# A Fourier filter and bilinear layer on one core: first batch in full rows of d, output stored in two halves of tokens

## The chip, the cores and the metric

The kernel runs on one core of one Trainium2 chip. The time is device microseconds of one execution of the whole program. All data is float32, and the matmuls of the main part are made exact enough by splitting operands into a high and a low part.

## The reference, cut to what matters

```python
# x [8, 3072, 256], filt_r / filt_i [1537, 256], w_a / w_b [256, 1536], w_out [1536, 256]
X = np.fft.rfft(x, axis=1)
y = np.fft.irfft(X * (filt_r + 1j * filt_i), n=3072, axis=1)
y = y.reshape(8 * 3072, 256)
out = ((y @ w_a) * (y @ w_b)) @ w_out
```

The weights arrive as float64 bit patterns and are converted on the chip.

## The kernel before, in words

**Filter.** The transform of the 3072 tokens is done in two stages of matmuls (3072 = 128 x 24). Stage one of the first batch is `first_s1` (12 items), whose result goes to HBM in `z0`; it comes back in another layout (`first_z`), goes through stage two, the product with the filter and the first inverse stage (`first_s2` and `first_is1`, 16 turns), and is put into HBM in `td`. The last inverse stage (`is2`) reads it from there (tile `tt`) with a table `gt` and leaves the operand pair `ah`, `al` for 512 tokens, one chunk. The first batch has its own functions (`first_*`, L437 to L509), which work on halves of d: 12 items are 2 halves of 128 columns by 6 groups of four n, and 16 turns are 2 halves by 8 groups. Rows of 128 float32 (512 bytes) are what its transfers carry.

**Weights.** Eighteen pieces of the weights are loaded and split by a pipeline, `more_weights` (L653): one call, here named a tick, loads piece t and does the five later stages of the pieces before it. In the before kernel six ticks are called ahead of and inside the loop of `first_s1`, six in the loop over the turns, and eleven in the first slots of the main part.

**Main part.** Eight batches of six chunks c, each with twelve slots f (L764 to L788). A slot is numbered 12 * c + f in its batch. In each slot `hidden` makes two products of 512 tokens with 128 hidden columns, `product` multiplies them on DVE into `g`, and `project` multiplies by `w_out` with a seven-product scheme into PSUM tiles `po`. The work for the next batch and the next chunk (loads, transform stages) is put into slots by hand with `at(slot, fn, ...)`, L715 to L763. Two entries matter here: `load_t` for the first chunk of the next batch stands in slot 68, which is c = 5, f = 8, and the two `is2` that need it in slots 69 and 70 (L761 to L763); and in batch 0 `load_s` of item i + 2 stands in slot 14 + i, and `s1` of the same item two slots later (L738, L743). The order of instructions on an engine is the order in which this program calls them, and SP's queue, which issues nearly all loads, has one such order as well.

**Output.** When a chunk's products are complete, `combine_first` (f = 2) and `combine` (f = 3 of the next chunk) add them up into `ct`, and `store` (f = 5) transposes `ct` in 32 x 32 blocks on DVE into `ot` and issues sixteen DMAs of 32 KB each from SP. After the last chunk the same is done with nothing beside it (L789 to L797).

Of the kernel before, what the change touches and what calls it, by code (L numbers as in the profile page):

```python
# [19 lines left out]
N1, N2 = 128, 24  # L20
# [175 lines left out]
def fft_filter_bilinear_kernel(ctx: ExitStack, tc, x, filt, fny, wa, wb, wo, s1c, gc, fc, fl, ic, sc, s1f, ff, fi, out):  # L196
# [240 lines left out]
    side = [slice(0, 128), slice(128, 256)]  # L437

# [5 lines left out]
    def first_x(h, i):  # L444
        xt = fr.tile([128, 4, 128], F32, name="x0", tag="in", bufs=9)
        nc.sync.dma_start(out=xt, in_=x[0].rearrange("(p n) d -> p n d", n=N2)[:, 4 * i:4 * i + 4, side[h]])
        held["x0", h, i] = xt

    def first_s1(h, i):
        xt, sf = held.pop(("x0", h, i)), held["sf", i // 2]  # L450
        bank, tag = ((ps_h, "pa"), (ps_h, "pb"), (ps_o, "po0"), (ps_o, "po1"))[i % 4]
        ps = bank.tile([128, 4, 128], F32, name="ps", tag=tag)
        for n in range(4):
            nc.tensor.matmul(ps[:, n], sf[:, 4 * (i % 2) + n], xt[:, n], start=True, stop=True)
        z = fr.tile([128, 4, 128], F32, name="z0", tag="z0", bufs=3)
        nc.scalar.copy(out=z, in_=ps)
        nc.scalar.dma_start(out=z0[:, 4 * i:4 * i + 4, side[h]], in_=z)

    def first_f(h, i):
        ft = filts[(8 * h + i) % NFT].rearrange("p j (h d) -> p (j h) d", h=2)  # L460
        nc.sync.dma_start(out=ft, in_=filt[:, 4 * i:4 * i + 4, side[h]])
        held["f0", h, i] = ft

    def first_z(h, i):
        zt = fr.tile([128, 4, 128], F32, name="zf", tag="in", bufs=9)
        zv = z0.rearrange("(j q) n d -> j (q n) d", q=4)[4 * i:4 * i + 4, :, side[h]]
        nc.sync.dma_start(out=zt[0:96], in_=zv.rearrange("j p d -> p j d"))
        held["z0", h, i] = zt

    def first_turn(i, w, ins, ps):  # L470
        for j0, j1, kind in ((0, 1, 1), (1, 4, 0)) if i == 0 else ((0, 4, 0),):
# [3 lines left out]
    def first_s2(h, i):  # L475
        zt, ft = held.pop(("z0", h, i)), held.pop(("f0", h, i))
        bank, tag = ((ps_h, "pa"), (ps_h, "pb"), (ps_o, "po0"), (ps_o, "po1"))[i % 4]
        ps = bank.tile([128, 4, 128], F32, name="ps", tag=tag)
        first_turn(i, fcf, [zt[0:96]], ps)
        y = fr.tile([128, 4, 128], F32, name="y0", tag="y", bufs=3)  # L480
        v = fr.tile([128, 4, 128], F32, name="v0", tag="v", bufs=3)
        xi = fr.tile([128, 4, 128], F32, name="xi", tag="xi")
        nc.vector.tensor_tensor(out=y[0:64], in0=ps[0:64], in1=ft[0:64], op=ALU.mult)
        nc.vector.tensor_tensor(out=y[64:128], in0=ps[64:128], in1=ft[0:64], op=ALU.mult)
        nc.vector.tensor_tensor(out=v[64:128], in0=ps[0:64], in1=ft[64:128], op=ALU.mult)
        nc.scalar.mul(out=xi[64:128], in_=ps[64:128], mul=-1.0)
        nc.gpsimd.tensor_tensor(out=v[0:64], in0=xi[64:128], in1=ft[64:128], op=ALU.mult)
        if i == 0:
            nc.vector.tensor_tensor(out=y[64:65, 0], in0=ps[64:65, 0], in1=nyq[64:65, side[h]], op=ALU.mult)
        held["y0", h, i] = [y, v]  # L490

    def first_is1(h, i):
        ps = ps_f.tile([128, 4, 128], F32, name="ps", tag="ff")[0:96]
        first_turn(i, icf, held.pop(("y0", h, i)), ps)
        t = fr.tile([96, 4, 128], F32, name="t0", tag="t")
        nc.scalar.copy(out=t, in_=ps)
        tv = td[0].rearrange("(j q) n d -> j (q n) d", q=4)[4 * i:4 * i + 4, :, side[h]]
        nc.scalar.dma_start(out=tv.rearrange("j p d -> p j d"), in_=t)
# [9 lines left out]
    def first_tt(h):  # L508
        nc.sync.dma_start(out=held["t", 0, 0][0][:, :, side[h]], in_=td[0][:, 0:4, side[h]])  # L509
# [113 lines left out]
    def combine(b, c):  # L623
        (m5, m4), (m7, m6) = ((t[:, 0], t[:, 1]) for t in po.pop((b, c))[2:])
        ct, u1, u4, _ = sums.pop((b, c))
        u2 = moe[0].tile([128, 256], F32, name="u2", tag="u2")
        u3 = moe[0].tile([128, 256], F32, name="u3", tag="u3")
        for o, v, w, op in (
            (u2, m6, u1, ALU.add), (u3, m7, u2, ALU.add), (ct[:, 1, 0], u3, m4, ALU.subtract),
            (ct[:, 1, 1], m5, u3, ALU.add), (u2, m5, u2, ALU.add), (ct[:, 0, 1], u2, u4, ALU.add),  # L630
        ):
            nc.vector.tensor_tensor(out=o, in0=v, in1=w, op=op)
        sums[b, c] = ct

    def store(b, c):
        ct = sums.pop((b, c))

        ot = moe[0].tile([128, 16, 2, 32], F32, name="ot", tag="ot")
        for h in range(2):
            nc.vector.transpose(ot[:, :, h], ct[:, h].rearrange("p t (j c) -> p (t j) c", c=32))  # L640

        ov = out[S * b:S * b + S].rearrange("(j c n) d -> c n j d", j=4, c=32)[:, 4 * c:4 * c + 4]
        for i in range(4):
            for n in range(4):
                nc.sync.dma_start(  # L645
                    out=ov[:, n, :, 64 * i:64 * i + 64],
                    in_=ot[32 * i:32 * i + 32, 4 * n:4 * n + 4].rearrange("p j h r -> p j (h r)"),
                )


    with tc.manual_schedule():
# [9 lines left out]
        items = [(h, i) for h in range(2) for i in range(6)]  # L661
        turns = [(h, i) for h in range(2) for i in range(8)]
# [8 lines left out]
        for n in range(6, 8):  # L671
            first_x(*items[n])
        for n, item in enumerate(items):
            first_s1(*item)
            if n + 8 < len(items):
                first_x(*items[n + 8])
            if n == 4:
# [4 lines left out]
            if n in (1, 3):  # L682
                more_weights()
            if 5 <= n < 9:
                first_f(*turns[n - 5])
                first_z(*turns[n - 5])
            if n in (7, 10):
                more_weights()
        for n in range(NJ + 2):
            if n < NJ:  # L690
                first_s2(*turns[n])
            if n + 4 < NJ:
                first_z(*turns[n + 4])
            if NFT <= n + NFT - 1 < NJ:
                first_f(*turns[n + NFT - 1])
            if n >= 2:
                first_is1(*turns[n - 2])
            if n % 2 == 1 and tick[0] < 12:
                more_weights()
            if n == 13:  # L700
# [11 lines left out]
        for b in range(B):  # L712
# [6 lines left out]
            if b == 0:  # L719
# [4 lines left out]
                at(10, nc.sync.dma_start, s1d, s1c)  # L724
# [39 lines left out]
            for c in range(NC):  # L764
                for f in range(NF):
# [19 lines left out]
                    if f == 5 and last[0] >= 0:  # L785
                        store(*last)
# [9 lines left out]
        combine(*last)  # L796
        store(*last)  # L797
# [34 lines left out]
```

## Time and profile before

| | |
|---|---|
| median of 3 runs | 2778.95 us (2777.82 to 2781.3) |
| the profiled execution's own time | 2778.72 us |
| its span in the trace | 2776.9 us |
| mean granted TensorE clock | 0.984 |
| PE busy | 2686.4 us (97%) |
| DVE / ACT / POOL busy | 1653.3 (60%) / 1304.2 (47%) / 1645.5 us (59%) |
| PE in 40 slices | 6 7 7 8, then 9 in all but the last |

PE is TensorE; DVE, ACT and POOL are the vector, scalar and GpSimd engines, SP the engine whose queue issues the loads and stores. An entry "SPq" or "ACTq" is the issuing of a DMA. In a row of a timeline the number in square brackets is the idle time of the engine before the instruction, with what ended it. The PE clock has two levels, 1.2 and 2.4 GHz, shown as 0.50 and 1.00.

### The profile page before, as it was taken

The numbers are of one execution on the slowest core, as the hardware profiler recorded it, in microseconds if no ns is written. First come the engines' busy times: TensorE is split into PE (matmuls) and PEld (weight loads), VectorE is DVE, ScalarE is ACT, GpSimd is POOL, SyncE is SP. The second block draws the span as 40 slices with busy tenths as digits, with TensorE's granted clock in tenths as the row PEclk, the third lists the DMA queues.
The fourth block names the chain that finished last, engine by engine and source line by source line (L and its number), as shares of the span: only waits on it lengthen the run. The fifth ranks groups of instructions, "written<-read, shape, count | busy, mean of one in ns | idle before, by whom it ended". The sixth has DMA issues, their size and how long they took to land.

```text
span 2776.9 us, 43491 instructions
## 1 busy us (share of the span) xinstructions
PE 2686.4 (97%) x14926; PEld 2299.4 (83%) x14926; DVE 1653.3 (60%) x2673; ACT 1304.2 (47%) x2711; POOL 1645.5 (59%) x1419
## 2 busy tenths in 40 slices
PE   6778999999999999999999999999999999999997
PEld 3467888888888888888888888888888888888886
DVE  5765775457744577446764477545774457744443
ACT  3444444445445454454444444454454544444343
POOL 3576565666656566566666566565665656655554
PEclk8889999999999999999999999999999999999998
DMA  9526452445424443343433545144532444320110
GB/s 269 144 93 202 132 137 58 129 131 139 114 71 130 144 129 89 100 155 114 140 82 99 157 112 143 49 138 130 139 109 72 146 127 133 81 50 20 24 23 16
DMA packets 331233, 310.27 MB, mean 112 GB/s; under 512 B 130449, under 2 KB 258002, under 8 KB 330962
## 3 DMA queue, kind: packets, MB, share of 16 engines
q1 hardware_dynamic: 266354, 227.32, 30.1%
q10 hardware_dynamic: 64256, 79.71, 8.5%
q8 instruction: 118, 1.93, 0.3%
q14 instruction: 105, 0.86, 0.1%
q0 software_dynamic: 400, 0.44, 0.1%
HBM read 202.49 MB, written 108.00 MB: 112 GB/s over the span
## 4 chain that ended last, share of the span: by engine, by line
PE 85%; issue 3%; POOL 2%; DVE 1%; SPq 1%; DMA 1%; ACT 0%; POOLq 0%; DVEq 0%; ACTq 0%
PE pb L541 9%; PE pb L542 9%; PE pb L543 9%; PE pa L543 9%; PE pa L542 9%; PE pa L541 9%; PE po L600 8%; PE po L598 8%; PE po L599 8%; PE ps L524 3%; PE ps L364 2%; PE ps L399 2%; POOL gl L581 2%; PE ps L398 2%; SPq L645 1%
## 5 line engine op out<-in xcount | busy, mean ns | idle before, releaser
L581 POOL TENSOR_TENSOR gl<-g,gh 128x256 fp32r<-128x256 f32 x576 | 573.9, 1018 | 990.9 <-ACT gh L580 878.8
L551 DVE TENSOR_TENSOR g<-pb,a 128x512 f32<-128x512 f32 x576 | 398.2, 691 | 839.9 <-PE pb L543 436.0
L581 POOL TENSOR_TENSOR gl<-t,gh 128x512 fp32r<-128x512 f32 x576 | 754.0, 1331 | 32.2 <-ACT gh L580 32.2
L547 ACT COPY a<-pa 128x512 f32<-128x512 f32 x576 | 338.2, 587 | 495.3 <-PE pa L543 481.8
L600 PE MATMUL po<-gl,woh 128*128 128x256 f32 x2016 | 568.7, 282 | 1.2 <-POOL gl L581 1.2
L598 PE MATMUL po<-gh,woh 128*128 128x256 f32 x2016 | 568.5, 282 | 1.0 <-ACT gh L580 1.0
L599 PE MATMUL po<-gh,wol 128*128 128x256 f32 x2016 | 568.2, 282 | 0.0
L541 PE MATMUL pb<-ah,wbh 128*128 128x512 f32 x1152 | 462.0, 401 | 15.0 <-DVE g L551 13.3
L541 PE MATMUL pa<-ah,wah 128*128 128x512 f32 x1152 | 465.8, 404 | 6.4 <-ACT a L547 6.3
L542 PE MATMUL pb<-al,wbh 128*128 128x512 f32 x1152 | 457.9, 397 | 0.0
L543 PE MATMUL pa<-ah,wal 128*128 128x512 f32 x1152 | 457.6, 397 | 0.0
L542 PE MATMUL pa<-al,wah 128*128 128x512 f32 x1152 | 457.4, 397 | 0.0
L543 PE MATMUL pb<-ah,wbl 128*128 128x512 f32 x1152 | 457.4, 397 | 0.0
L580 ACT CAST gh<-t 128x512 fp32r<-128x512 f32 x576 | 328.6, 618 | 193.2 <-PE po L599 190.6
L598 PEld LDWEIGHTS po<-gh,woh 128*128 128x128 f32 x2016 | 380.0, 188 | 27.5 <-ACT gh L580 1.2
L599 PEld LDWEIGHTS po<-gh,wol 128*128 128x128 f32 x2016 | 380.5, 189 | 26.2
L600 PEld LDWEIGHTS po<-gl,woh 128*128 128x128 f32 x2016 | 381.3, 189 | 1.8 <-POOL gl L581 1.8
L541 PEld LDWEIGHTS pb<-ah,wbh 128*128 128x128 f32 x1152 | 218.1, 189 | 82.4 <-DVE g L551 28.9
L580 ACT CAST gh<-g 128x256 fp32r<-128x256 f32 x576 | 266.8, 513 | 0.0
L543 PEld LDWEIGHTS pb<-ah,wbl 128*128 128x128 f32 x1152 | 217.8, 189 | 53.6
L543 PEld LDWEIGHTS pa<-ah,wal 128*128 128x128 f32 x1152 | 217.8, 189 | 51.7
L542 PEld LDWEIGHTS pb<-al,wbh 128*128 128x128 f32 x1152 | 217.9, 189 | 50.4
(98 smaller groups left out, 3325.7 us busy)
## 6 DMA issues: line engine op xcount, KB each, us to landing
filt<-in_filt SPq DMA_DIRECT2D x336, 128.0 KB, 3.5
z<-zh ACTq DMA_DIRECT2D x112, 256.0 KB, 2.4
zt<-z SPq DMA_DIRECT2D x112, 256.0 KB, 3.0
td<-t ACTq DMA_DIRECT2D x128, 192.0 KB, 2.3
out<-ot SPq DMA_DIRECT2D x768, 32.0 KB, 1.6
tt<-td SPq DMA_DIRECT2D x47, 512.0 KB, 5.4
xt<-in_x SPq DMA_DIRECT2D x84, 256.0 KB, 3.2
st<-s1d SPq DMA_DIRECT2D x84, 256.0 KB, 4.3
```

The costliest lines, as they stand in the source:

```text
L364: nc.tensor.matmul(ps[:, n], st[:, n, w], m[:, n], start=q == 0, stop=q == 2)
L524: nc.tensor.matmul(ps[:, n], tt[:, n, 128 * k:128 * k + 128], gt[:, n], start=True, stop=True)
L541: nc.tensor.matmul(p, wh[:, k, fs], ah[:, k], start=k == 0, stop=False)
L542: nc.tensor.matmul(p, wh[:, k, fs], al[:, k], start=False, stop=False)
L543: nc.tensor.matmul(p, wl[:, k, fs], ah[:, k], start=False, stop=k == 1)
L547: nc.scalar.copy(out=a, in_=pa)
L551: nc.vector.tensor_tensor(out=raw[0][:, 2 * i:2 * i + 2].rearrange("p t n -> p (t n)"), in0=pb, in1=a, op=ALU.mult)
L580: nc.scalar.copy(out=gh[:, e], in_=g[:, e])
L581: nc.gpsimd.tensor_tensor(out=gl[:, e], in0=g[:, e], in1=f32(gh[:, e]), op=ALU.subtract)
L598: nc.tensor.matmul(o, woh[:, p, w], gh, start=first, stop=False, skip_group_check=True)
L599: nc.tensor.matmul(o, wol[:, p, w], gh, start=False, stop=False, skip_group_check=True)
L600: nc.tensor.matmul(o, woh[:, p, w], gl, start=False, stop=last, skip_group_check=True)
```

## The change

Three things change. First, the first batch works on full rows of d: an item is two n by 256 columns, a turn two j by 256, so that the same 12 items and 16 turns move rows of 1 or 2 KB, and the nyquist row is done once instead of twice. The loads of all items come ahead of the first weights; four ticks, not six, lie in the loop of the items, and eight in the loop of the turns. A turn now needs `z0` of all twelve items, where it needed that of six. `tt` of the first chunk is loaded by halves of its partitions, no longer by halves of d. Second, the two transposes and sixteen stores of a chunk are cut by halves of tokens t: two transposes of half the width and eight stores in slot f = 5, the same again in f = 7. Third, after the last chunk the first half is transposed and stored as soon as its sums are there, and the stores go alternately to SP's and ACT's queue.

```diff
-    def first_x(h, i):
-        xt = fr.tile([128, 4, 128], F32, name="x0", tag="in", bufs=9)
-        nc.sync.dma_start(out=xt, in_=x[0].rearrange("(p n) d -> p n d", n=N2)[:, 4 * i:4 * i + 4, side[h]])
...
+    def first_x(i):
+        xt = fr.tile([128, 2, D], F32, name="x0", tag="in", bufs=9)
+        nc.sync.dma_start(out=xt, in_=x[0].rearrange("(p n) d -> p n d", n=N2)[:, 2 * i:2 * i + 2])
...
+    def first_z(i):
+        zt = fr.tile([128, 2, D], F32, name="zf", tag="in", bufs=9)
+        zv = z0.rearrange("(j q) n d -> j (q n) d", q=4)[2 * i:2 * i + 2]
...
     def first_tt(h):
-        nc.sync.dma_start(out=held["t", 0, 0][0][:, :, side[h]], in_=td[0][:, 0:4, side[h]])
+
+        nc.sync.dma_start(out=held["t", 0, 0][0][half[h]], in_=td[0][half[h], 0:4])
...
-    def combine(b, c):
+    def combine(b, c, end=False):
...
             (u2, m6, u1, ALU.add), (u3, m7, u2, ALU.add), (ct[:, 1, 0], u3, m4, ALU.subtract),
+            (None, 0, 0, 0),
             (ct[:, 1, 1], m5, u3, ALU.add), (u2, m5, u2, ALU.add), (ct[:, 0, 1], u2, u4, ALU.add),
         ):
-            nc.vector.tensor_tensor(out=o, in0=v, in1=w, op=op)
-        sums[b, c] = ct
...
+            if o is not None:
+                nc.vector.tensor_tensor(out=o, in0=v, in1=w, op=op)
+            elif end:
+                store(b, c, ct, ot, 0, end)
+        sums[b, c] = ct, ot
+        if end:
+            store(b, c, ct, ot, 1, end)
+
+    def store(b, c, ct, ot, t, end=False):
+
         for h in range(2):
-            nc.vector.transpose(ot[:, :, h], ct[:, h].rearrange("p t (j c) -> p (t j) c", c=32))
+            nc.vector.transpose(ot[:, 8 * t:8 * t + 8, h], ct[:, h, t].rearrange("p (j c) -> p j c", c=32))
...
-        for i in range(4):
-            for n in range(4):
-                nc.sync.dma_start(
+        for n in (2 * t, 2 * t + 1):
+            for i in range(4):
+                (nc.scalar if end and i % 2 else nc.sync).dma_start(
...
-        for n in range(3):
+        for n in range(2):
             first_const(n)
-            first_x(*items[2 * n])
-            first_x(*items[2 * n + 1])
-        for n in range(2):
-            more_weights()
...
+            for i in range(4 * n, 4 * n + 4):
+                first_x(i)
+        first_const(2)
+        first_x(8)
...
-            if n in (1, 3):
+            if n in (2, 4, 6, 9):
                 more_weights()
...
+            if n in (7, 8):
+                first_f(n - 7)
+        for n in range(4):
+            first_z(n)
+            if n < 2:
+                first_f(n + 2)
...
-                at(10, nc.sync.dma_start, s1d, s1c)
+                at(7, nc.sync.dma_start, s1d, s1c)
...
-                    if f == 5 and last[0] >= 0:
-                        store(*last)
+                    if f in (5, 7) and last[0] >= 0:
+                        store(*last, *sums[last], f // 2 - 2)
...
-        combine(*last)
-        store(*last)
+        combine(*last, end=True)
```

At the passage from batch 0 to batch 1, DVE (`g` is the product of a slot, the three `t` are the differences of each odd slot, `ot` the transposes of the store, `al` the end of `is2`) has this order before, from f = 5 on:

```order
L640 STREAM_TRANSPOSE ot<-ct 128x16x32 x2
L551 TENSOR_TENSOR g<-pb,a 128x512 x2
L560 TENSOR_TENSOR t<-g 128x512
L561 TENSOR_TENSOR t<-g,t 128x256
L562 TENSOR_TENSOR t<-t,g 128x256
L551 TENSOR_TENSOR g<-pb,a 128x512 x2
L560 TENSOR_TENSOR t<-g 128x512
L561 TENSOR_TENSOR t<-g,t 128x256
L562 TENSOR_TENSOR t<-t,g 128x256
L527 TENSOR_TENSOR al<-ps,ah 128x512
```

and this one with the change:

```order
L646 STREAM_TRANSPOSE ot<-ct 128x8x32 x2
L552 TENSOR_TENSOR g<-pb,a 128x512 x2
L561 TENSOR_TENSOR t<-g 128x512
L562 TENSOR_TENSOR t<-g,t 128x256
L563 TENSOR_TENSOR t<-t,g 128x256
L646 STREAM_TRANSPOSE ot<-ct 128x8x32 x2
L552 TENSOR_TENSOR g<-pb,a 128x512 x2
L561 TENSOR_TENSOR t<-g 128x512
L562 TENSOR_TENSOR t<-g,t 128x256
L563 TENSOR_TENSOR t<-t,g 128x256
L528 TENSOR_TENSOR al<-ps,ah 128x512
```

Half of the transposes now stand behind the products and differences of f = 6 and 7. SP's queue at the same place, with the change:

```order
L651 DMA out<-ot 32x4x64 x16
L514 DMA tt<-td 128x1024
L516 DMA gt<-in_gc 128x512
L343 DMA xt<-in_x 128x2x256 x3
L348 DMA st<-s1d 128x512 x2
```

The row of sixteen stores reads as it did before, and `tt` and `gt` follow it as before; but its last eight now wait for the second pair of transposes.

In chunk 1 of batch 0, where the loads `xt` and `st` of the next batch are under way, SP's queue before is

```order
L348 DMA st<-s1d 128x512
L645 DMA out<-ot 32x4x64 x16
L343 DMA xt<-in_x 128x2x256
L348 DMA st<-s1d 128x512
L343 DMA xt<-in_x 128x2x256
L348 DMA st<-s1d 128x512
```

and with the change

```order
L348 DMA st<-s1d 128x512
L651 DMA out<-ot 32x4x64 x8
L343 DMA xt<-in_x 128x2x256
L348 DMA st<-s1d 128x512
L343 DMA xt<-in_x 128x2x256
L348 DMA st<-s1d 128x512
L651 DMA out<-ot 32x4x64 x8
```

Two pairs of loads now stand ahead of the second eight stores.

## Rows read from the trace of the kernel before

**Rows 1.** PE from 260 to 2750 us: busy time by stretch, then its waits there

```profile
260.00:2750.00 2490.00, 2481.13 (x14036) 2148.71 (x14035) 1485.45 (x2411) 1184.36 (x2483) 1492.88 (x1286) 1.00 0.37 106
...
PE pb L541 <- DVE g L551: 5.8, 15, 0.4
PE ps L524 <- DMA gt<-in_gc: 1.3, 3, 0.7
```

**Rows 2.** Timelines of SP, DVE and PE where batch 0 passes to batch 1

```profile
465.37 0.43 SPq L515 DMA_DIRECT2D gt<-in_gc  x1
...
462.18 0.43 DVE L562 TENSOR_TENSOR t<-t,g 128x256 f32<-128x256 f32 x1
...
469.98 1.13 PE L524 MATMUL ps<-gt,tt 128*128 128x128 f32 x8 [0.73 <-DMA gt<-in_gc]
```

**Rows 3.** The same timelines where batch 1 passes to batch 2

```profile
785.45 7.45 SPq L645 DMA_DIRECT2D out<-ot  x16
793.42 0.43 SPq L515 DMA_DIRECT2D gt<-in_gc  x1
...
791.57 0.42 DVE L562 TENSOR_TENSOR t<-t,g 128x256 f32<-128x256 f32 x1
...
798.48 1.05 PE L524 MATMUL ps<-gt,tt 128*128 128x128 f32 x8
```

**Rows 4.** Timeline of PE: first instructions after three of its idle times

```profile
127.59 0.80 PE L541 MATMUL pb<-ah,wbh 128*128 128x512 f32 x1 [3.56 <-DVE g L551]
...
155.19 0.50 PE L541 MATMUL pb<-ah,wbh 128*128 128x512 f32 x1 [1.40 <-DVE g L551]
...
190.22 0.50 PE L541 MATMUL pa<-ah,wah 128*128 128x512 f32 x1 [2.08 <-ACT a L547]
```

**Rows 5.** Stretches behind them: PE, PEld, DVE, ACT, POOL busy, PE clock, DMA share

```profile
132.00:133.00 1.00, 1.00 (x6) 0.86 (x5) 0.96 (x2) 0.00 (x0) 0.29 (x1) 0.58 0.89 172
155.00:156.00 1.00, 0.81 (x4) 0.69 (x5) 1.00 (x3) 0.97 (x3) 1.00 (x2) 1.00 0.00 0
191.00:192.00 1.00, 1.00 (x4) 0.71 (x4) 0.92 (x2) 0.00 (x0) 1.00 (x3) 0.50 0.00 0
194.00:195.00 1.00, 1.00 (x6) 0.82 (x6) 0.08 (x1) 0.15 (x1) 1.00 (x2) 0.86 1.17 360
```

**Rows 6.** Timelines of SP and PE in batch 0, chunk 1, around f = 5

```profile
223.77 8.02 SPq L645 DMA_DIRECT2D out<-ot  x16
232.38 0.41 SPq L348 DMA_DIRECT2D st<-s1d  x1
...
235.65 0.55 PE L364 MATMUL ps<-xh,st 128*128 128x256 f32 x1 [7.62 <-DMA st<-s1d]
```

**Rows 7.** The end: timeline of DVE and SP, then a stretch of the stores

```profile
2766.01 1.30 DVE L640 STREAM_TRANSPOSE ot<-ct 128x512 f32<-128x512 f32 x2
2767.35 7.43 SPq L645 DMA_DIRECT2D out<-ot  x16
...
2769.00:2771.00 2.00, 0.00 (x0) 0.00 (x0) 0.00 (x0) 0.00 (x0) 0.00 (x0) 0.50 0.41 66
```

**Rows 8.** Transfers of the first 40 us: GB/s by slice, and their packets

```profile
GB/s 0 45 152 383 323 252 241 347 345 359 350 306 365 416 404 367 343 332 307 271 294 324 280 344 395 372 358 354 205 116 310 225 229 251 240 261 319 374 390 349
DMA packets 16759, 11.90 MB, mean 297 GB/s; under 512 B 761, under 2 KB 15606, under 8 KB 16758
```

**Rows 9.** Timeline of DVE, then PE: turns 0, 3, 4 and 15 of the first batch, then `is2`

```profile
40.70 0.68 DVE L483 TENSOR_TENSOR y<-ps,filt 64x512 f32<-64x512 f32 x1
...
51.92 0.68 DVE L483 TENSOR_TENSOR y<-ps,filt 64x512 f32<-64x512 f32 x1
...
56.77 0.68 DVE L483 TENSOR_TENSOR y<-ps,filt 64x512 f32<-64x512 f32 x1
...
99.00 0.68 DVE L485 TENSOR_TENSOR v<-ps,filt 64x512 f32<-64x512 f32 x1
...
109.72 2.04 PE L524 MATMUL ps<-gt,tt 128*128 128x128 f32 x8 [5.83 <-DMA tt<-td]
```

More of the change, by code (lines that the diff above doesn't have):

```diff
@@ L434, in is1 @@
         nc.scalar.dma_start(out=tv.rearrange("j p d -> p j d"), in_=t)
-    side = [slice(0, 128), slice(128, 256)]
     def first_const(n):
@@ L459, in first_f @@
[L459 to L466, printed above, removed]
+    def first_x(i):
+        xt = fr.tile([128, 2, D], F32, name="x0", tag="in", bufs=9)
+        nc.sync.dma_start(out=xt, in_=x[0].rearrange("(p n) d -> p n d", n=N2)[:, 2 * i:2 * i + 2])
+        held["x0", i] = xt
@@ new lines, in fft_filter_bilinear_kernel, with first_s1 @@
+    BANKS = ((ps_h, "pa"), (ps_h, "pb"), (ps_o, "po0"), (ps_o, "po1"))
+    def first_s1(i):
+        xt, sf = held.pop(("x0", i)), held["sf", i // 4]
+        bank, tag = BANKS[i % 4]
+        ps = bank.tile([128, 2, D], F32, name="ps", tag=tag)
+        for n in range(2):
+            nc.tensor.matmul(ps[:, n], sf[:, 2 * (i % 4) + n], xt[:, n], start=True, stop=True)
+        z = fr.tile([128, 2, D], F32, name="z0", tag="z0", bufs=3)
+        nc.scalar.copy(out=z, in_=ps)
+        nc.scalar.dma_start(out=z0[:, 2 * i:2 * i + 2], in_=z)
@@ L467, in first_z, with first_f @@
+    def first_f(i):
+        ft = filts[i % NFT]
+        nc.sync.dma_start(out=ft, in_=filt[:, 2 * i:2 * i + 2])
+        held["f0", i] = ft
+    def first_z(i):
+        zt = fr.tile([128, 2, D], F32, name="zf", tag="in", bufs=9)
+        zv = z0.rearrange("(j q) n d -> j (q n) d", q=4)[2 * i:2 * i + 2]
         nc.sync.dma_start(out=zt[0:96], in_=zv.rearrange("j p d -> p j d"))
-        held["z0", h, i] = zt
+        held["z0", i] = zt
     def first_turn(i, w, ins, ps):
-        for j0, j1, kind in ((0, 1, 1), (1, 4, 0)) if i == 0 else ((0, 4, 0),):
+        for j0, j1, kind in ((0, 1, 1), (1, 2, 0)) if i == 0 else ((0, 2, 0),):
@@ L488, in first_s2, with first_is1 @@
         if i == 0:
[L489 to L495, printed above, removed]
+            nc.vector.tensor_tensor(out=y[64:65, 0], in0=ps[64:65, 0], in1=nyq[64:65], op=ALU.mult)
+        held["y0", i] = [y, v]
+    def first_is1(i):
+        ps = ps_f.tile([128, 2, D], F32, name="ps", tag="ff")[0:96]
+        first_turn(i, icf, held.pop(("y0", i)), ps)
+        t = fr.tile([96, 2, D], F32, name="t0", tag="t")
         nc.scalar.copy(out=t, in_=ps)
-        tv = td[0].rearrange("(j q) n d -> j (q n) d", q=4)[4 * i:4 * i + 4, :, side[h]]
+        tv = td[0].rearrange("(j q) n d -> j (q n) d", q=4)[2 * i:2 * i + 2]
         nc.scalar.dma_start(out=tv.rearrange("j p d -> p j d"), in_=t)
@@ L627, in combine @@
         u3 = moe[0].tile([128, 256], F32, name="u3", tag="u3")
+        ot = moe[0].tile([128, 16, 2, 32], F32, name="ot", tag="ot")
         for o, v, w, op in (
             (u2, m6, u1, ALU.add), (u3, m7, u2, ALU.add), (ct[:, 1, 0], u3, m4, ALU.subtract),
+            (None, 0, 0, 0),
             (ct[:, 1, 1], m5, u3, ALU.add), (u2, m5, u2, ALU.add), (ct[:, 0, 1], u2, u4, ALU.add),
         ):
[L632 to L638 removed]
+            if o is not None:
[6 more added lines that the diff above has]
+    def store(b, c, ct, ot, t, end=False):
         for h in range(2):
[L640 removed]
+            nc.vector.transpose(ot[:, 8 * t:8 * t + 8, h], ct[:, h, t].rearrange("p (j c) -> p j c", c=32))
         ov = out[S * b:S * b + S].rearrange("(j c n) d -> c n j d", j=4, c=32)[:, 4 * c:4 * c + 4]
[L643 to L645 removed]
+        for n in (2 * t, 2 * t + 1):
+            for i in range(4):
+                (nc.scalar if end and i % 2 else nc.sync).dma_start(
                     out=ov[:, n, :, 64 * i:64 * i + 64],
@@ L660, in fft_filter_bilinear_kernel @@
         start_batch(0)
-        items = [(h, i) for h in range(2) for i in range(6)]
-        turns = [(h, i) for h in range(2) for i in range(8)]
         nc.vector.memset(cut[:, 0:1], float(1151 << 20))
         nc.vector.memset(cut[:, 1:2], float(255 << 23))
-        for n in range(3):
+        for n in range(2):
             first_const(n)
-            first_x(*items[2 * n])
-            first_x(*items[2 * n + 1])
-        for n in range(2):
-            more_weights()
[L671 to L677, printed above, removed]
+            for i in range(4 * n, 4 * n + 4):
+                first_x(i)
+        first_const(2)
+        first_x(8)
+        for n in range(NI):
+            first_s1(n)
+            if n + 9 < NI:
+                first_x(n + 9)
+            if n == 3:
                 nc.sync.dma_start(out=fcf, in_=ff)
```

38 lines of the change are left out of this document (12 added, 26 removed).

## The prediction

> **What bounds the kernel now.** I read the busy table and the slices of the page first: PE is full everywhere except in the first 260 us and at the very end. The stretch from 260 to 2750 us makes that exact, 2481.1 of 2490.0 us busy at full clock, and its list of waits is short: 5.8 us on DVE's product and 1.3 us, three times, on the table `gt` [rows 1]. So in the middle whatever keeps PE waiting goes straight into the time, and whatever it does not wait for is worth nothing. The timelines of SP, DVE and PE at the passages between batches show how close the one DMA wait is [rows 2, 3]; the waits of the first 260 us and the end are read from their own timelines [rows 6, 7, 9]. An effect of 0.2% (5.6 us) is about what a measurement of this kernel can tell from none.
>
> The profiled execution took 2778.72 us, 0.23 us under the median of 2778.95; its span is 2776.9 us. The sum is made against 2778.72 us.
>
> **The change part by part.**
>
> *The end, -5.4 us.* Before, sixteen issues on SP run for 7.43 us from 2767.35 us, when both transposes (1.30 us) are over, and the span ends 2.1 us after the last [rows 7]. With the change the first eight go out during the last three sums. The last eight start at about the same time as the first did, 0.1 us later for two more instructions, four on each queue: 4 x 0.464 = 1.9 us. Gain 7.43 - 1.9 - 0.1 = 5.4 us. The DMA engines had a share of 0.41 while one queue issued [rows 7]; two queues make 0.8 of it, so they should still keep up. If they do not, the gain falls towards 3.6 us (all eight from one queue, 3.7 us); if the receipt is quicker too, 6.
>
> The Trainium skill, "DMA: Bandwidth & Descriptors", section "Issuing engines are not separate DMA queues", says that issuing from several engines saves only the sequencer's time, which it calls usually small beside the DMA. Here the trace shows that time as the larger part; by the page's "usually small" the end would gain 3.6 us and the sum would be 1.8 us higher.
>
> *The stall in batch 0, -4.6 us.* At 235.65 us PE has waited 7.62 us for a table `st` whose load stood in SP's queue behind sixteen stores of 8.02 us; 3.3 us pass from its issue at 232.38 us to the matmul [rows 6]. With the change only eight stores (4.0 us) and half the transposes (0.65 us) are ahead of it: the matmul starts 4.6 us earlier. The second eight stand two pairs of loads later, and the load behind them is needed two slots on, so I add nothing. Bounds: -2 (some of it waits again in the next slots) to -5.5. About 3.0 us of waiting stay.
>
> *The passages between batches, +20.0 us of waiting.* This is the largest term. `gt` of the next batch is issued right behind the sixteen stores, at 465.37 us; the matmul that needs it starts 4.61 us later, at 469.98 us, after a wait of 0.73 us [rows 2]. In the next passage the issue is at 793.42 us, PE is ready at 798.48 us and does not wait, with some 0.4 us to spare [rows 3]. With the change the last eight stores need the transposes of f = 7. These stand behind `t` (L562), which starts at 791.57 us and lets the next instruction begin 0.35 us later; two half transposes take some 0.76 us (half of 1.30 and a start more [rows 7]), so the stores begin at 792.7 us. Eight at 7.45 / 16 = 0.466 us end at 796.4 us [rows 3]; `tt` takes the next 0.5 us and `gt` goes out at 796.95 us, 3.5 us later than before. It is there at 801.55 us: a stall of 3.1 us. In the first passage the same steps from 462.18 us give 472.2 us against a ready PE at 469.25 us, 2.95 us in place of 0.73. There are seven passages; the four without a wait before cost 3.1 us each, the three with one 2.95 us each less the 1.3 us they already had [rows 1]: 12.4 + 8.9 - 1.3 = 20.0 us. Nothing covers it: the engine that waits is the full one. If `gt` lands 0.6 us sooner it is 16; if the stores go at the 0.5 us each of rows 6, 22.
>
> *The clock behind these stalls, +11.2 us.* After an idle time of 1.40 us the clock stayed at 2.4 GHz; after 2.08 us it fell to 1.2 GHz and was not back until 194.1 us, some 3.2 us of work; after 3.56 us it stayed low until 132.6 us, 5 us [rows 4, 5]. A stall of 3 us lies between the last two, so I take the fall, at half of 3.2 us, 1.6 us each: 7 x 1.6 = 11.2 us. Below: nothing, if it holds; above: 2.5 us each, 17.5 us. The stall of batch 0 keeps its own low stretch, so nothing is gained there.
>
> *The first batch, +1.9 us.* DVE does turn after turn from 40.70 to 99.7 us [rows 9]. Three things move. First, the start of the turns. A turn needs all of `z0` now, so ahead of it go the tables (1.57 MB), x (3.15 MB), `z0` (3.15 MB), some three weight pieces (1.57 MB) and small tables, 9.8 MB. At the mean of the first 40 us, 297 GB/s in packets of mostly 512 bytes, that is 33.0 us, at 400 GB/s, which the slices reach, 24.5 us [rows 8]. With 2 us before data flows, 4.6 us for reading `z0` back (the landing of `gt` [rows 2]) and 1.5 us of matmuls, the first turn starts between 32.6 and 41.1 us; ACT's copies of `z0` wait in between for a weight piece, so I take 38.5, 2.2 us sooner than now. Second, eight ticks instead of six lie in the loop; the last falls behind the last turn, where DVE idles. One more is thus paid: from turn 3 to turn 4, with a tick, DVE takes 56.77 - 51.92 = 4.85 us [rows 9], against some 2.1 us for a turn's three instructions: 2.7 us, with a weight combination more, so +3.2 us. The second nyquist product goes, -1 us. Third, both `is2` now wait for the second half of `tt`, where only the second did: its four matmuls, 1.7 us of the 2.04 [rows 9], come behind that wait, and ACT's part of the last tick adds 0.5 us; the larger rows of `td` and `tt` give back 0.3. Sum: -2.2 + 3.2 - 1.0 + 1.7 + 0.5 - 0.3 = 1.9 us. Bounds: -4 and +5.
>
> The same skill page, section "Specifications", gives 512 bytes as the least transfer for line rate; by that the rows of 1 and 2 KB would bring nothing. With 33.0 us for the transfers the first turn starts at 41.1 us and the sum is 2.6 us higher.
>
> *No cost.* In other chunks the second pair of transposes adds some 0.76 us to DVE in f = 7; PE's whole wait for DVE there is 5.8 us in 2490 [rows 1], at other slots, and loads have four slots before they are needed. The copy of `s1d` moves from slot 10 to 7, but SP's order has the same neighbours on both sides, so nothing moves.
>
> **Sum:** -5.4 - 4.6 + 20.0 + 11.2 + 1.9 = +23.1 us, 2801.8 us: slower by 0.8%.
>
> **The rivals.**
>
> *The clock holds.* Then 11.2 us fall away: 2790.7 us. For it: a stall stands alone in full work, while the 2.08 us idle time followed others. Against it: no idle time over 2 us in the rows goes without a fall. Chance 0.2.
>
> *The passages hide the later loads: faster.* If `gt`, now behind eight stores and not sixteen, landed within 1.5 us of its issue instead of 4.6, PE would find it ready; from there on the passage costs nothing and the clock stays up. -5.4 - 4.6 + 1.9 - 1.3 = -9.4 us, 2769.3 us. For it: the stores ahead are fewer at once. Against: the DMA share during stores is only 0.41 [rows 7], so the 4.6 us are no queue of stores but the loads themselves. Chance 0.07.
>
> *The first batch is dearer.* If the wait for all of `z0` starts the turns at 45 us, that term is +8.4 us and the time 2808.4 us. For it: before, half of `z0` was enough. Against: less data in small packets. Chance 0.1.
>
> *The split order does not reach the chip as written.* The order of SP and DVE shows that it does; this would leave the end alone, 2773.3 us. Chance 0.03.
>
> **How the numbers follow.** The forecast of 2802 us has a chance of 0.6. The range reaches from the clock that holds, with an early `gt` (2786 us), to the dear first batch and longer low stretches (2811 us). Over 2784.5 us count the forecast, the first and the third rival and parts around them, 0.85; within 0.2%, mixtures of a hidden passage with a dear first batch, 0.07; faster, the second and part of the fourth rival, 0.08.
>
> **What would show it.** At each of the seven passages `gt` issued 3 to 3.5 us later and PE's wait for it near 3 us, some 21 us in all where there were 1.3, followed by a clock of 0.50; the wait for `st` in batch 0 near 3 us; the last store issued about 2 us after the last transpose; DVE's first turn at 36 to 41 us and the last near 100 us. The prediction is wrong if PE's waits for `gt` stay under 1 us a passage, or if the first hidden product starts more than 6 us from where it does now.

## The result and the profile after

The changed kernel takes **2803.24 us** (median of four runs, 2798.67 to 2806.91), the kernel before 2778.39 us beside it: a ratio of **1.0087**, 95% interval 1.007 to 1.0105. It is slower by 0.9%; the forecast was 2802 us. The profiled execution is the longest of the four, 2806.91 us with a span of 2804.9 us, so the terms read from it add up to 28.0 us of span where the medians differ by 24.9.

PE's waits in the middle of the changed kernel, from 260 to 2800 us (waiting instruction, releaser: us in total, times, longest). It answers to [rows 1]:

```profile
PE ps L525 <- DMA gt<-in_gc: 19.6, 7, 3.1
PE pb L542 <- DVE g L552: 5.4, 14, 0.4
```

The wait for DVE is as it was; the wait for `gt` has gone from 1.3 us to 19.6. SP's timeline at the second passage (start, us, instruction), with DVE's `t` at 796.76 us beside it, says how; it answers to [rows 3]:

```profile
797.90 3.65 SPq L651 DMA_DIRECT2D out<-ot  x8
801.64 0.38 SPq L514 DMA_DIRECT2D tt<-td  x1
802.06 0.43 SPq L516 DMA_DIRECT2D gt<-in_gc  x1
```

`gt` is issued 802.06 - 796.76 = 5.30 us behind `t`, where it was 793.42 - 791.57 = 1.85 us; PE's matmul starts 4.41 us after that, where it was 4.61 us at the first passage before [rows 2]. PE's first matmul behind each of the seven passages, idle time ahead of it in brackets:

```profile
472.42 2.05 PE L525 MATMUL ps<-gt,tt 128*128 128x128 f32 x8 [2.96 <-DMA gt<-in_gc]
806.47 2.04 PE L525 MATMUL ps<-gt,tt 128*128 128x128 f32 x8 [2.62 <-DMA gt<-in_gc]
1139.42 1.13 PE L525 MATMUL ps<-gt,tt 128*128 128x128 f32 x8 [2.87 <-DMA gt<-in_gc]
1472.41 2.05 PE L525 MATMUL ps<-gt,tt 128*128 128x128 f32 x8 [2.75 <-DMA gt<-in_gc]
1806.55 2.05 PE L525 MATMUL ps<-gt,tt 128*128 128x128 f32 x8 [2.66 <-DMA gt<-in_gc]
2139.41 1.13 PE L525 MATMUL ps<-gt,tt 128*128 128x128 f32 x8 [2.72 <-DMA gt<-in_gc]
2472.68 2.05 PE L525 MATMUL ps<-gt,tt 128*128 128x128 f32 x8 [3.06 <-DMA gt<-in_gc]
```

Stretches behind the first two of these passages (busy time of PE, PEld, DVE, ACT and POOL, then PE's granted clock, DMA share, GB/s):

```profile
476.00:478.00 2.00, 2.00 (x6) 1.61 (x5) 0.00 (x0) 0.94 (x4) 0.00 (x0) 0.50 0.04 8
478.00:480.00 2.00, 2.00 (x13) 1.75 (x13) 0.69 (x1) 0.56 (x2) 1.88 (x2) 0.89 0.00 0
808.00:810.00 2.00, 2.00 (x8) 1.68 (x8) 0.69 (x1) 0.59 (x1) 0.00 (x0) 0.62 0.55 202
810.00:812.00 2.00, 2.00 (x11) 1.63 (x11) 0.00 (x0) 1.50 (x4) 0.47 (x1) 1.00 0.00 0
```

Behind the first the clock stays at 1.2 GHz (0.50) for 6.0 us of work, to 478.4 us; behind the second for 3.1 us, to 809.5 us. In this execution all seven passages have such a stretch, three of 6.0 to 6.1 us and four of 3.1 to 3.4 us of work.

What this costs shows between the first hidden product of chunk 3 in batch 0 and the same one in batch 7, a stretch that holds all seven passages; before, then after:

```profile
313.64:2604.64 2291.00, 2282.70 (x12919) 1977.33 (x12918) 1385.09 (x2237) 1099.02 (x2297) 1384.03 (x1190) 1.00 0.39 110
313.87:2638.10 2324.23, 2297.93 (x12919) 1989.21 (x12918) 1390.83 (x2321) 1098.71 (x2297) 1384.00 (x1190) 0.99 0.38 109
```

It is 33.2 us longer, of which 18.3 us (19.6 - 1.3) are waiting for `gt`; some 14.9 us are left for the low clock.

The rest of the difference. In batch 0 the wait for `st` is 3.47 us at 235.69 us in place of 7.62 us [rows 6]. At the end, DVE, SP and ACT:

```profile
2796.53 0.88 DVE L636 TENSOR_TENSOR u<-po,u 128x256 f32<-128x256 f32 x2 [1.65 <-PE po L601]
...
2797.92 0.77 DVE L646 STREAM_TRANSPOSE ot<-ct 128x256 f32<-128x256 f32 x2
...
2798.72 3.75 SPq L651 DMA_DIRECT2D out<-ot  x8
2798.72 3.83 ACTq L651 DMA_DIRECT2D out<-ot  x8
...
2799.90 0.77 DVE L646 STREAM_TRANSPOSE ot<-ct 128x256 f32<-128x256 f32 x2
```

From the first of the last sums (2796.53 us) to the span's end pass 8.37 us; before, from 2763.38 us, 13.52 us: 5.15 us gained. The first batch, DVE's first turn, the last one's `v` and PE's `is2`, answering to [rows 9]:

```profile
40.40 0.68 DVE L483 TENSOR_TENSOR y<-ps,filt 64x512 f32<-64x512 f32 x1 [10.50 <-PE ps L473]
...
100.58 0.68 DVE L485 TENSOR_TENSOR v<-ps,filt 64x512 f32<-64x512 f32 x1
...
112.49 3.75 PE L525 MATMUL ps<-gt,tt 128*128 128x128 f32 x16 [7.76 <-DMA tt<-td]
```

PE's first hidden product starts at 115.90 us; before, at 111.42 us: 4.5 us lost.

So 18.3 us of waiting, some 14.9 us of low clock at the passages, 4.5 us in the first batch, less 4.15 us of the stall and 5.15 us of the end: 28.4 us, where the spans differ by 28.0.

### The profile page after: what moved, and what is told of

Same layout as the page of the kernel before. It is cut to its first block, busy times and chain, and to the rows that moved or that the text cites. A ratio compares the mean times of both kernels' runs of the same rounds, so it can differ in the third digit from the quotient of the medians.

```text
span 2804.9 us, 43537 instructions
## 1 busy us (share of the span) xinstructions
PE 2697.7 (96%) x14872; PEld 2304.2 (82%) x14872; DVE 1659.8 (59%) x2768; ACT 1304.1 (46%) x2711; POOL 1646.4 (59%) x1419
## 4 chain that ended last, share of the span: by engine, by line
PE 84%; issue 3%; DVE 2%; POOL 2%; DMA 1%; SPq 1%; POOLq 0%; ACT 0%; DVEq 0%; ACTq 0%
PE pb L542 9%; PE pb L544 9%; PE pb L543 9%; PE pa L544 9%; PE pa L543 9%; PE pa L542 9%; PE po L601 8%; PE po L599 8%; PE po L600 8%; PE ps L525 3%; PE ps L364 2%; PE ps L399 2%; PE ps L398 2%; POOL gl L582 2%; DMA gt<-in_gc 1%
## 5 line engine op out<-in xcount | busy, mean ns | idle before, releaser
L542 PE MATMUL pb<-ah,wbh 128*128 128x512 f32 x1152 | 463.5, 402 | 15.3 <-DVE g L552 13.4
```

The costliest lines, as they stand in the source:

```text
L542: nc.tensor.matmul(p, wh[:, k, fs], ah[:, k], start=k == 0, stop=False)
```

## The experiments

Each run stood beside runs of the kernel before on the same chip; what it is "over" or "under before" is its median less theirs, so that runs made at different times can be set side by side. "Loads ahead" is the changed kernel with the edit of the first experiment.

### The passages: `gt`'s place in SP's queue

```diff
-                    at(12 * c + 3 if c + 1 < NC else 68, load_t, nb, ncx)
+                    at(12 * c + 3 if c + 1 < NC else 66, load_t, nb, ncx)
```

> Of the changed kernel only the slot is changed in which the next batch's first tt and gt are loaded: 66 in place of 68, so that both loads stand between the two groups of eight stores on SP instead of behind them. Theory 1 (gt's place in SP's queue is the whole loss of the passages, the clock falls because of that wait): PE's waits for gt fall from 19.6 us to 1.3 us or less, the clock stays at 1.00 through all seven passages, and the time falls by the 18.3 us of waiting and some 14.6 us of low clock to 2770 to 2775 us, under the kernel before. Theory 2 (the transposes in f = 7 or the split of the stores cost the time, wherever gt stands): waits and low stretches stay and the time stays within 5 us of 2803 us. Between them: if only part of the waiting goes (gt lands late because the stores of the first half are still moving), 2780 to 2795 us.

Measured: 2770.7 us, 5.45 us under before, ratio 0.9979 (0.9971 to 0.9988). The time of the passages is thereby 24.85 + 5.45 = **30.3 us**. SP at the first passage, then PE there:

```profile
456.18 3.65 SPq L651 DMA_DIRECT2D out<-ot  x8
459.93 0.38 SPq L514 DMA_DIRECT2D tt<-td  x1
460.35 0.43 SPq L516 DMA_DIRECT2D gt<-in_gc  x1
463.96 3.66 SPq L651 DMA_DIRECT2D out<-ot  x8
...
469.74 1.06 PE L525 MATMUL ps<-gt,tt 128*128 128x128 f32 x8
```

PE's list of waits for this kernel has no `gt` in it, and the clock is 1.00 behind all seven passages. The transposes in f = 7 and the split stores are all still there, and cost nothing: theory 1 holds, theory 2 falls.

**Both halves in f = 5**, of the changed kernel:

```diff
-                    if f in (5, 7) and last[0] >= 0:
-                        store(*last, *sums[last], f // 2 - 2)
+                    if f == 5 and last[0] >= 0:
+                        store(*last, *sums[last], 0)
+                        store(*last, *sums[last], 1)
```

> Of the changed kernel only the slot of the second eight stores in the middle is changed: both halves are stored in f = 5, sixteen stores in a row as before the change; the first batch and the end stay as changed. Theory 1 (only the order on SP counts): waits for gt back to about 1.3 us over the seven passages, no low clock there, and the stall of batch 0 for st back from 3.5 to about 7.6 us; the time is that of the kernel before plus 4.2 us for the first batch less 5.2 us for the end, 2777 to 2778 us. Theory 2 (transposes by halves of tokens, 4 instructions in place of 2, are what costs): the time stays over 2795 us. The difference of this run to the one with the loads ahead measures the stall of batch 0 alone, 4.2 us expected.

Measured: 2774.46 us, 1.69 us under before, ratio 0.9993 (0.9984 to 1.0002); no wait for `gt` in the list, and in batch 0 PE waits 7.07 us for `st` again. The old order on SP with the new half transposes is as good as before, so the order is what costs. Against the run with the loads ahead it is 3.8 us longer: the stall of batch 0, 4.15 us in the traces of before and after, 2.9 us in those of these two runs (7.07 - 4.2).

### The clock at the passages

Eight matmuls that fill the idle time, in the changed kernel, `gt` left where the change puts it:

```diff
+    def fill(b, c):
+        ah = held["t", b, c][2]
+        ps = ps_f.tile([128, 512], F32, name="ps", tag="ff")
+        for q in range(8):
+            nc.tensor.matmul(ps, wah[:, 0, 0:128], ah[:, 0], start=q == 0, stop=q == 7)
...
+                    if c + 1 == NC:
+                        at(69, fill, b, c)
```

> The changed kernel with eight more matmuls of 512 columns (some 1.9 us of PE, their result is read by nobody) on PE in slot 69 of each passage between batches, just ahead of the matmuls that wait for gt. The order on SP and DVE is left as it is. Theory 1 (part of the loss is the granted clock behind an idle time of 2.6 to 3.1 us): PE now idles some 0.9 us at each passage, the clock stays at 1.00, waiting plus added work is as long as the waiting was, and the time falls by the clock's share, 10 to 15 us, to 2788 to 2793 us, although work was added. Theory 2 (the clock costs nothing that the waits don't hold already): the time stays within 3 us of 2803 us. Theory 3 (the low clock has another cause than the idle time): the clock still falls, and the time is 2803 us or up to 13 us more.

Measured: 2792.06 us, 15.9 us over before, ratio 1.0053 (1.0039 to 1.0066), 8.9 us less than the changed kernel's 24.85; 10 to 15 us less were expected. PE's remaining wait, and the clock behind the first passage:

```profile
PE ps L525 <- DMA gt<-in_gc: 6.3, 7, 1.3
...
472.00:478.00 6.00, 5.90 (x39) 5.39 (x40) 1.38 (x2) 2.65 (x7) 1.99 (x2) 1.00 0.49 172
```

The clock is 1.00 in the same stretch behind each of the seven passages. PE has 56 more matmuls, and the kernel is faster. Waiting and fill (6.3 us, and some 13 us at 0.235 us from one matmul's start to the next) together are as long as the waiting was, so what went is the clock's share: theory 1, with a size of 9 us in the medians. By the profiled executions it is more, 2806.91 - 2792.27 = 14.6 us, since the profile of the changed kernel is of its longest run. A second profile of the changed kernel follows.

> The changed kernel, unaltered, on the chip and in the call of the three runs beside it, for a second profile. Its first four runs spread over 8.2 us where the kernel before spreads over 4.3 us, and the profile was taken on the slowest. Theory 1 (the clock's fall behind a wait near 3 us isn't certain, and a run's time follows from the number of passages at which it falls): this profile again shows waits for gt of 18 to 20 us in all, and low stretches at some or all of the seven passages, each passage without one making the run 1.6 to 3.1 us shorter than 2806.9 us. Rival (the spread lies in the first batch or the loads): seven low stretches of the same lengths, and the difference of the two runs before 260 us.

Measured: 2801.34 us (2797.81 to 2805.08), 24.4 us over before, ratio 1.0089 (1.0075 to 1.0103). Its waits and, behind the second and the seventh passage, its clock:

```profile
PE ps L525 <- DMA gt<-in_gc: 20.5, 7, 3.9
...
805.19 1.13 PE L525 MATMUL ps<-gt,tt 128*128 128x128 f32 x8 [2.62 <-DMA gt<-in_gc]
...
805.00:807.00 2.00, 1.81 (x12) 1.71 (x13) 0.03 (x1) 0.58 (x1) 0.00 (x0) 1.00 1.07 373
807.00:809.00 2.00, 2.00 (x11) 1.59 (x10) 0.67 (x1) 1.25 (x4) 0.19 (x1) 1.00 0.43 159
2471.00:2473.00 2.00, 2.00 (x9) 1.91 (x9) 0.00 (x0) 0.18 (x1) 0.00 (x0) 0.50 0.00 0
2473.00:2475.00 2.00, 2.00 (x6) 1.60 (x5) 0.69 (x1) 0.41 (x1) 0.00 (x0) 0.50 0.00 0
```

Behind an idle time of 2.62 us the clock does not fall here; in the first profile it fell behind the same 2.62 us. Of the seven passages one has no low stretch, four have one of 2.8 to 3.4 us of busy PE, two one of 5.7 and 6.2 us. The run with the loads ahead does the same work at full clock, so PE's busy time in the stretch from batch 0 to batch 7 tells the cost: with the loads ahead, then in this second profile,

```profile
314.33:2603.04 2288.71, 2281.85 (x12919) 1977.25 (x12918) 1390.01 (x2321) 1098.52 (x2297) 1382.73 (x1190) 1.00 0.38 111
314.41:2636.29 2321.88, 2295.22 (x12920) 1987.00 (x12918) 1389.93 (x2321) 1098.25 (x2297) 1383.28 (x1190) 0.99 0.38 109
```

against 2297.93 us in the first profile: 16.1 us in the first and 13.4 us in the second (15.2 and 12.5 us against the 2282.70 us of the kernel before). The two executions differ by 2.4 us in this stretch, and by 1.9 us in their spans, so theory 1 of this run holds and not the rival. That the whole spread of 7 us comes from the clock is not shown, since only two executions have a profile.

### The end: one queue or two

Loads ahead, with all stores on SP:

```diff
-                (nc.scalar if end and i % 2 else nc.sync).dma_start(
+                nc.sync.dma_start(
```

> The changed kernel with the loads of tt and gt in slot 66, and with all sixteen stores of the very end issued on SP instead of on SP and ACT in turn. By the prediction's price of an issue (0.464 us) the last eight take 3.7 us in place of 1.9 us, and the first eight, 3.7 us long from the first half's transposes on, may still be going when the second half's transposes are over, 2.0 us later: the second eight then start some 1.8 us later too. Expected: the end 1.8 to 3.6 us longer, 2772.5 to 2774.3 us against 2770.7 us. Rival (the last transfer's own time sets the end, not the issuing): no difference, 2770.7 us within 1 us.

Measured: 2774.22 us, 2.74 us under before, ratio 0.999 (0.9982 to 0.9999): 2.7 us longer than with two queues. DVE and SP of this kernel:

```profile
2760.38 0.89 DVE L636 TENSOR_TENSOR u<-po,u 128x256 f32<-128x256 f32 x2 [1.83 <-PE po L601]
...
2762.57 7.43 SPq L651 DMA_DIRECT2D out<-ot  x16
...
2763.74 0.77 DVE L646 STREAM_TRANSPOSE ot<-ct 128x256 f32<-128x256 f32 x2
```

SP issues sixteen without a gap and ends at 2770.00 us, 2.1 us ahead of the span's end: the issuing sets the end. From 2760.38 us to the end are 11.72 us against 8.37 with two queues. So in the traces 1.8 us of the 5.15 come from the first eight's earlier start and 3.35 from the second queue; in the medians the second queue is worth 2.7 us.

### The first batch

**The old first batch**: the kernel before with the stores and the end of the change, and with the loads in slot 66.

> The kernel before with its own first batch, with the stores by halves of tokens and the two queues at the end of the change, and with the next batch's first tt and gt loaded in slot 66. Theory 1 (the changed first batch costs 4.2 us by itself, the end gains 5.2 us, the stall of batch 0 4.2 us, and the passages cost nothing once gt stands ahead of the second eight stores): 2778.4 - 5.2 - 4.2 = 2769 us, 4 us under the same kernel with the changed first batch. Rival (the first batch's later first product is paid back further on, by a stall that is shorter for it): the same time as that kernel, within 1.5 us. If the passages' one wait of 0.7 us goes too, 2767 us.

Measured: 2765.18 us, 10.97 us under before, ratio 0.9959 (0.9946 to 0.9971), 5.5 us under the same kernel with the changed first batch; 4 us were expected. The rival, that the later first product is paid back further on, falls. PE's first hidden product is at 112.15 us here, at 117.58 us in the other, 5.4 us later. Of the six profiled executions with the changed first batch as it is, four have it at 115.75 to 115.91 us and two, both with the loads ahead, at 117.58 and 117.62 us; in those two the granted clock was 0.50 from 100 to 106 us, in the four 0.72 or 1.00, and ACT's last copy ahead of the last `td` store waited 1.8 us for PE. So some 4 to 5.5 us is what the first batch costs. The end (5.15), the stall (4.15) and the 1.3 us of waits for `gt` before make 10.6 of the 10.97 us.

**A fourth `z0` buffer**, loads ahead:

```diff
-        z = fr.tile([128, 2, D], F32, name="z0", tag="z0", bufs=3)
+        z = fr.tile([128, 2, D], F32, name="z0", tag="z0", bufs=4)
```

> The changed kernel with the loads of tt and gt in slot 66, and with four buffers in place of three for the first batch's z0 tiles, so that ACT's copies wait less often for the landing of a store. Theory A (ACT's waits for these landings, 3.3, 3.3 and 3.1 us, set when the first turn of DVE starts): one wait in four goes or shrinks, DVE's first turn starts 1 to 3 us before 40.6 us, and the time is 1 to 3 us under the 2770.7 us of the same kernel with three buffers. Theory B (the transfers themselves set it, x, tables, weight pieces and z0 at the rate of the DMA engines): ACT waits less at one place and more at the next, the first turn stays within 0.7 us of 40.6 us, and the time within 1 us.

Measured: 2769.59 us, 7.37 us under before, ratio 0.9972 (0.9961 to 0.9984). In the run with three buffers ACT's copies of `z0` waited for a landing of its own stores so:

```profile
14.57 0.59 ACT L456 COPY z<-ps 128x512 f32<-128x512 f32 x1 [3.31 <-DMA z<-z]
...
20.84 0.59 ACT L456 COPY z<-ps 128x512 f32<-128x512 f32 x1 [3.30 <-DMA z<-z]
...
32.00 0.59 ACT L456 COPY z<-ps 128x512 f32<-128x512 f32 x1 [3.06 <-DMA z<-z]
```

With four, waits of 0.71 and 2.52 us are left, and DVE's first turn starts at 38.67 us in place of 40.61: theory A by the trace, with the same bytes to move. In the time, 1.9 us, the intervals overlap.

**Two early weight ticks in place of four**, loads ahead:

```diff
-            if n in (2, 4, 6, 9):
+            if n in (2, 4):
```

> The changed kernel with the loads of tt and gt in slot 66, and with two weight ticks in place of four in the first batch's first loop (the ones behind its seventh and tenth step fall into the loop of turns and behind it). Theory B (transfers set the start of the turns): the loads and conversions taken out of the stretch before 38 us, 1.6 to 2.1 MB less at the 297 GB/s of the kernel before, let the first turn start 3 to 5 us sooner; one more tick among the turns costs DVE 2.7 to 3.2 us, so the first hidden product comes 0 to 2 us sooner and the time is 2768.5 to 2771 us, unless later weight pieces are late in batch 0, which would show as waits of PE before 260 us. Theory A (ACT's waits for z0 landings set it): the first turn moves by under 1 us, the tick costs its 3 us, and the time is 2773 to 2775 us.

Measured: 2764.49 us, 12.47 us under before, ratio 0.9955 (0.9942 to 0.9967), 7.0 us under four early ticks and more than either theory gave. The first turn starts at 37.49 us, 3.1 us sooner, as theory B has it. (A tick takes its transfers and its work on ACT and DVE out of this stretch together, so the run doesn't tell which of them counted.) But the turns are shorter too, 52.6 us from first to last where they were 60.1. DVE's groups of instructions in the turns (count, busy us, mean ns, then idle time), with four early ticks, 40 to 101 us:

```profile
L249 DVE TENSOR_SCALAR e<-raw 128x512 int32<-128x512 int32 x7 | 6.9, 983 | 0.0
L269 DVE SCALAR_TENSOR_TENSOR sc<-raw,sc 128x512 int32<-128x512 int32 x7 | 4.9, 705 | 0.2
```

and with two, 37 to 91 us:

```profile
L269 DVE SCALAR_TENSOR_TENSOR sc<-raw,sc 128x512 int32<-128x512 int32 x6 | 4.3, 716 | 0.2
...
L249 DVE TENSOR_SCALAR e<-raw 128x512 int32<-128x512 int32 x7 | 4.0, 576 | 0.0
```

A tick in the loop is not worth a full tick there: the pieces are two stages behind, so one piece less is split ahead of the last turn, and the two weight combinations (L305, 2.4 us) fall behind it. The same seven L249 cost 2.9 us less as well. Single rows, with four early ticks, say why:

```profile
63.47 0.42 DVE L249 TENSOR_SCALAR e<-raw 128x512 int32<-128x512 int32 x1
63.48 1.53 POOL L287 TENSOR_TENSOR m<-m,wah 128x512 f32<-128x512 f32 x1
...
77.43 1.26 POOL L284 TENSOR_TENSOR m<-m,e 128x512 f32<-128x512 f32 x1
77.47 1.51 DVE L249 TENSOR_SCALAR e<-raw 128x512 int32<-128x512 int32 x1
```

Where POOL's instruction was already running, L249 took 1.27 to 1.52 us and ended 0.3 us behind it: four of the seven. Where L249 began first, it took 0.42 to 0.44 us, and POOL's took 1.50 to 1.53 us instead of some 1.26. With two early ticks one of the seven is of the long kind, and the next three long ones (94.44, 100.86 and 104.91 us) come behind the turns. The expectation had priced a moved tick as a tick more. The rest of what left the turns is done behind them, where the next run looks.

**The second half of `tt` ahead of the last tick**, with two early ticks:

```diff
+        first_tt(1)
         while tick[0] < 12:
             more_weights()
-        first_tt(1)
```

> The kernel with the loads of tt and gt in slot 66 and two early weight ticks, and in it the load of the second half of tt ahead of the last tick behind the loop of turns. In the run before, this load went out at 101.53 us, behind two raw weight loads that held SP from 94.55 us on, while the last store of td had been issued at 96.39 us. Theory (SP's queue, not td, holds the load there): it goes out at 98.5 to 99.5 us, some 2.0 to 2.4 us behind the last store of td as in the kernel before, the first hidden product comes 2 to 3 us sooner, and the time is 2761.5 to 2763 us against 2764.5 us. Rival (the raw loads that now stand behind it come late for batch 0): the gain is given back as waits of PE before 260 us, 2764 to 2766 us.

Measured: 2761.89 us, 15.43 us under before, ratio 0.9945 (0.9933 to 0.9957), 3.0 us less. In the run before, SP had

```profile
94.55 6.80 SPq L244 DMA_DIRECT2D raw<-in_wo  x2
101.53 0.46 SPq L510 DMA_DIRECT2D tt<-td  x1
```

with the last `td` store issued at 96.39 us; now the load goes out at 101.01 us, 3.45 us behind a last store at 97.56 us, and the first hidden product starts at 108.22 us, not 109.66. The theory's direction holds; the 2.4 us it expected behind the store do not. The trace moved 1.4 us at the first hidden product where the medians differ by 3.0, and the two profiled executions have the same span (2760.0 and 2759.9 us), the run before being profiled at its fastest. The intervals overlap, so how much of the 3.0 us is this edit's isn't shown.

**And four `z0` buffers besides:**

> As the run with the second half of tt ahead of the last tick, and with four z0 buffers besides. With three buffers and two early ticks ACT still waits for landings of z0 (3.5, 3.1, 1.7 and 3.4 us) before the turns. Theory A (these waits are on the path to the first turn): the first turn starts 1.5 to 2 us sooner, as it did with four early ticks, and the time is 1 to 2 us under the run beside it. Theory B (with two early ticks the filter piece, for which DVE's first turn waited in that run, or the transfers decide): within 0.7 us of the run beside it.

Measured: **2758.16 us**, 19.16 us under before, ratio 0.9933 (0.9919 to 0.9946). The first turn is at 35.54 us (37.27 in the run beside it), the first hidden product at 106.09 us, 2.1 us sooner: theory A. The medians fell by 3.7 us where 1 to 2 were expected; the intervals overlap, and what the rest is isn't shown. It is the fastest kernel of this study, faster than both before and after.

**No early ticks** (three buffers, `tt` behind the ticks):

> The kernel with the loads of tt and gt in slot 66 and no weight tick at all in the first batch's first loop; nine of the twelve fall into the loop of turns and three behind it. If what the two ticks taken out brought (6 us) goes on in the same way, the first turn starts 2 to 3 us sooner again and the time falls to 2759 to 2762 us. Rival (behind the turns the ticks stand in the way instead: each holds the second half of tt on SP and the weights of the first hidden product): the first hidden product comes later by the ticks' DVE time, 3 us or more for each, and the time is 2765 to 2772 us.

Measured: 2764.54 us, 12.78 us under before, ratio 0.9954 (0.9942 to 0.9967): no more than two early ticks, above the 2759 to 2762 us expected and just under the rival's 2765 to 2772. The turns start at 34.35 and end with a `v` at 84.47 us, 5.6 us sooner, but the second half of `tt` waits again for raw loads:

```profile
96.26 5.61 SPq L244 DMA_DIRECT2D raw<-in_wo  x2
102.04 0.46 SPq L510 DMA_DIRECT2D tt<-td  x1
```

with the last `td` store at 90.32 us. The first hidden product starts at 110.25 us, 0.6 us later than with two early ticks: the gain of the turns is lost in SP's queue, the place that the rival names. This kernel with `tt` ahead of the ticks was not tried.

## Why the prediction was right, and where it was not

**The end, -5.4:** -5.15 us, from the two steps it names, the issues during the last sums and the second queue. Its price for the last eight on one queue was off: it left a gain of 3.6 us, and the run shows 1.8, because the first eight still hold SP when the second half is transposed. The Trainium skill ("DMA: Bandwidth & Descriptors", "Issuing engines are not separate DMA queues") calls the sequencer's time usually small beside the DMA; here the second queue alone brought 3.35 us in the traces and 2.7 us in the medians, so for these sixteen stores of 32 KB the measurement decides against "usually small".

**The stall in batch 0, -4.6:** -4.15 us by the trace, 3.8 us by the run with both halves in f = 5.

**The passages, +20.0 us of waiting:** +18.3 in the first profile, 19.2 in the second. The place (`gt` behind eight stores that wait for DVE's f = 7), the price (`gt` 5.38 us behind `t`, measured 5.30) and the proof (moved ahead, all of it goes) are as predicted.

**The clock, +11.2 us:** 16.1 and 13.4 us in the two profiled executions, which are the longest of their runs, about 9 by the fill, and 10 to 11 in the medians (30.3 us less a waiting of 19.6 or 20.5). In the medians the size was right, its model was not: not 1.6 us at each passage, but nothing, about 1.6 or about 3 us (half of the low stretch), differently in each execution. By rows 5 the low stretches that the prediction read end at 132.84 and 194.28 us, not 132.6 and 194.1 (a clock of 0.58 in one us is 0.84 us at half), which changes nothing in the sum. The rival "the clock holds" is out as a whole, though it held at one passage in fourteen.

**The first batch, +1.9 us:** +4.5, within its bounds of -4 and +5 but mis-sized, and the step that failed is the first: the turns were to start at 38.5 us and start at 40.40, 1.9 us of the 2.6. The working named ACT's wait for a weight piece and missed its waits for the landings of the `z0` stores, which the trace of after shows at 2.8 to 3.2 us three times and which a fourth buffer removes in part. By the Trainium skill ("DMA: Bandwidth & Descriptors", "Specifications") rows over 512 bytes would bring nothing. The prediction's sum by that, 41.1 us, is nearer to what was measured; but the same transfers with one more buffer start the turns at 38.67 us, so it was not the rate alone that held them. The other steps: one tick more less one nyquist product, +2.2 predicted, 60.18 - 58.30 = +1.9 measured; the tail from the last turn's `v` to the load of `tt`, +0.2 predicted, +0.65 measured; both `is2` behind that load, +1.7 predicted, from 4.88 to 7.13 us, +2.25 measured. The rival "the first batch is dearer" did not come about: it has the turns start at 45 us, and they start 0.3 us sooner than before.

**`s1d` in slot 7, 0:** it goes out at 149.98 us, 3.9 us later than before, as everything behind the first batch does.

The errors cancelled in part: waiting 1.7 us too much, the first batch 2.6 too little, the stall and the end 0.7 too much gain. That puts the median within 1.3 us of the forecast, which is closer than the parts deserve and in part luck; the profiled execution, with more low clock, is 28.0 us longer, 4.9 over the sum.

## What to carry to other kernels

When a transfer is split so that its second part waits for a later event, look at what stands behind that part on the same issuing queue: here two loads that had nothing to do with the stores were held 3.5 us, and moving them ahead of the second part turned 0.9% slower into 0.2% faster. Where the full engine idles for such a wait, price the granted clock behind it too: it made up 30 to 45% of the passages' cost, and differed from execution to execution. A step that is moved within a pipeline of stages has no fixed price: moving a tick into the loop shortened the loop, because the stages behind it moved out at its end; in the traces fewer of its instructions also began while POOL was busy.

## What the runs showed that was not expected

The same idle time of 2.62 us ended once with a granted clock of 0.50 and once of 1.00 in two executions of one program; the low stretches that followed idle times of 2.4 to 4.0 us came in two lengths, 2.8 to 3.4 and 5.7 to 6.2 us of busy PE. Work that nobody reads, put into these idle times, made the kernel 8.9 us faster. And one DVE instruction form on tiles of one size (L249) took 0.42 us or 1.27 to 1.52 us, as it began before an instruction of POOL or behind it; no run changed that order alone, so the cause is read from the traces only.
